# A Fourier mixing layer and a leaky-ReLU MLP on one core: the first rows of x loaded in fp32, loads and banks reordered, and one more chunk computed by Strassen

## The chip, the core and the metric

The kernel runs on one core of one Trainium2 chip. The metric is the device time of one execution in microseconds (us), the median of several runs. TensorE (PE) multiplies matrices and writes its results to PSUM banks. VectorE (DVE), ScalarE (ACT) and GpSimd (POOL) work on tiles. SyncE (SP) and POOL issue the DMA transfers of this kernel, and ACT issues a few at the very end.

## The reference, cut to what matters

```python
def _attn_ref(x, filt_r, filt_i):            # x: (8, 3008, 256) float32
    X = np.fft.rfft(x, axis=1)
    Y = X * (filt_r + 1j * filt_i)[None, :, :]
    return np.fft.irfft(Y, n=x.shape[1], axis=1)

def _moe_ref(x, w_in, w_out):                # x: (24064, 256)
    h = x @ w_in                             # (256, 2048)
    g = np.maximum(0.01 * h, h)
    return g @ w_out                         # (2048, 256)
```

The output of the first function, seen as 24064 tokens, is the input of the second.

## The kernel before, in words

The Fourier transform of length 3008 = 94 x 32 is done as matrix products in fp16, in four stages for each of the eight sequences (`b` = 0 to 7). Stage s1 multiplies the 94 rows of x by a small matrix (`fwd1`). A transposition follows. Stage s2 multiplies by the 24 matrices of `f2_sb`, and the spectrum is multiplied by the filters `fa_sb` and `fb_sb`. Stage sa multiplies by a small inverse matrix, a second transposition follows, and stage sb multiplies by the matrices of `i1_sb` and writes the mixed tokens `yt`. The MLP then works on chunks of 512 tokens: 32 matmuls of 512 columns with `w_in_sb` into the PSUM pair `ph` (L502), a leaky ReLU on ACT (L507) into `gt_c`, and the product with `w_out_sb`. There are 47 chunks.

The second product has two forms. `plain` (L623) does 64 matmuls of 256 columns per chunk (L627) and four copies on DVE (L632). `products` (L595) does Strassen's seven products of half-sized blocks: 112 matmuls of 128 columns (L566), with four sums of activations on DVE (L539), one copy on ACT (L603) and six additions on DVE (L591 to L619). The weight sums `wt_sb` are built once (L655). Chunks below `W0` = 3 are plain, the others Strassen (L711).

The first sequence is a prologue. Its order is written out by hand in the list `FIRST`, step by step: `s1p` matmuls of s1 on rows n0 to n0+n into a bank b0 to b4 (L367), `s1e` the copy of that bank to SBUF on ACT (A) or DVE (D) (L373), `t1` a quarter of the transposition on DVE (L376), `s2p` (L381), then the filter product either directly on DVE (`s2d`, L398) or by a copy on ACT (`s2a`, L401) and a multiplication on POOL (`s2m`, L408), `sap` and `sae` (L413, L418), `t2` (L422), `sbp` and `sbe` (L436, L439), and `warm n`, which issues n matmuls of 512 columns that nobody reads (L362). The banks b0, b1, b2 are single PSUM banks `pf`, b3 and b4 are the pairs `ph`. Each engine runs its own instructions in the order of the list.

What the prologue loads: SP issues the small matrices and two thirds of `f2_sb` (L205 to L207). POOL issues the first sequence of x in four parts of 10, 10, 8 and 4 rows, cast from fp32 to fp16 by the DMA (`x_load`, L188), then the filters with the last third of `f2_sb` between them (L211 to L216), then `w_in_sb`. In the middle of `FIRST` the step `i1` loads `i1_sb` on SP and the step `x` loads the next sequence of x in two halves with `w_out_sb` between them on POOL (`load_x`, L451).

From the second sequence on, the order is made by a planner. Each group of work gets a planned time in units of which 8 are one chunk (`SL`). `PLANS` gives starts and steps of the stages per sequence, `SUMS`, `REST`, `DUE`, `TWICE`, `F2T`, `LEAD`, `AFTER`, `LANDED` give times of single steps and distances between them. A heap sorts them, and the instructions are issued in that order on every engine. A group of s2 (`s2_group`, L293) multiplies one bank by both filters on DVE. In sequence 1 every even group does three DVE operations (L305, L306, L311). The odd groups and all later ones do two (L308, L311) and have two DMAs on SP swap the halves of p2 into p3 (L309, L310). POOL then adds p1 and p3 into y (L314). The tiles p1, p2 and p3 come from the pool `scrp` with two buffers each:

```python
p1, p2, p3 = (scrp.tile([P, 2, D], FP32, tag=f"p{i}", name=f"p{i}_b{b}_g{g}") for i in (1, 2, 3))
```

A group of sa (L321) reads y, its copy goes to ACT (L323), and its store to DRAM to SP (L325). The groups of s1 (L250), s2, sa and sb (L342) share the banks pf0 and pf1 in turn, and DVE and ACT empty them. The transpositions of sequences 1 to 7 go through DRAM (stores L255 and L325, loads L262 and L269).

Of the kernel before, what the change touches and what calls it, by code (L numbers as in the profile page):

```python
# [75 lines left out]
def kernel(  # L76
# [9 lines left out]
    nc = tc.nc  # L86
    B, N, D = x.shape
# [8 lines left out]
    SL = 8  # L96
    NCH = NCT // 2
    QT = 4 * N1
    W0 = 3
    GAP = 0.6  # L100
    EXG = 0
    LANDED = 2.43
    READ = 2.2
    SUMS = (0.09, 1.59, 2.35, 4)
    REST = (5.37, 14.61, 8.86, 10.48, 23.53, 20.72)
    DUE = (3.52, 0.66)
    TWICE = (1.43, 1.84)
    F2T = 3.24
    LEAD = (3.85, 7.37)
    AFTER = (0.53, 0.8, 1.33, 3.17, 0.39, 0.52)  # L110


    PLANS = (
# [4 lines left out]
    )  # L118

    f2_np, i1_np, small_np, f2t_np, i1t_np = _build_np_constants(N)  # L120
    f2_d = nc.inline_tensor(f2_np, name="fwd2_const")
# [6 lines left out]
    f2_sb = cpool.tile([P, NC, P], FP16, name="f2_sb")  # L128
# [5 lines left out]
    w_out_sb = cpool.tile([P, NCT, D], FP16, name="w_out_sb")  # L134
    wt_sb = cpool.tile([P, 4, NCH, P], FP16, name="wt_sb")
    x_sb = cpool.tile([P, N2, D], FP16, name="x_sb")
    big = [cpool.tile([P, Q * D], FP16, name=f"big{i}") for i in range(3)]
# [1 line left out]

    gtp = ctx.enter_context(tc.tile_pool(name="gtp", bufs=2))  # L140
    drp = ctx.enter_context(tc.tile_pool(name="drp", bufs=1, space=bass.MemoryType.DRAM))
    scrp = ctx.enter_context(tc.tile_pool(name="scr", bufs=2))
    ypp = ctx.enter_context(tc.tile_pool(name="ypp", bufs=4))
    outp = ctx.enter_context(tc.tile_pool(name="outst", bufs=4))
    psp = ctx.enter_context(tc.tile_pool(name="psp", bufs=1, space=bass.MemoryType.PSUM))
# [29 lines left out]
    def noted(what, f):  # L175
        f()
        issued.add(what)

    def soon(delay, f):
        at(clock["now"] + delay, f)  # L180
# [7 lines left out]
    def x_load(b, n0=0, nn=N2, d0=0, dn=D):  # L188

        for lo, cnt in ((0, R1),) if b + 1 < B else ((0, 64), (64, N1 - 64)):  # L190
            nc.gpsimd.dma_start(
                x_sb[lo : lo + cnt, ds(n0, nn), ds(d0, dn)],
                bass.AP(tensor=x.tensor, offset=x.offset + (b * N + lo * N2 + n0) * D + d0,
                        ap=[[N2 * D, cnt], [D, nn], [1, dn]]))
# [7 lines left out]
                        ap=[[N1 * D, N2 // 2], [sgn * NC * D, 2], [sgn * D, NC], [1, dn]]))  # L202


    nc.sync.dma_start(small_sb[:], small_d.ap())  # L205
    for i in (1, 0):
        nc.sync.dma_start(f2_sb[:, ts(i, NC // FP), :], f2_d.ap()[i])  # L207
    first_parts = ((0, 10), (10, 10), (20, 8), (28, 4))
    for n0, nn in first_parts:
        x_load(0, n0, nn)  # L210
    for hf in range(2):  # L211

        filt_load(0, filt_r, hf * DH, DH)
        filt_load(64, filt_i, hf * DH, DH)
        if hf == 0:
            nc.gpsimd.dma_start(f2_sb[:, ts(2, NC // FP), :], f2_d.ap()[2])  # L216
    nc.gpsimd.dma_start(w_in_sb[:], moe_w_in.rearrange("(dt p) c -> p dt c", p=P))
    idle = cpool.tile([P, CH], FP16, name="idle")
    nc.vector.memset(idle[:], 0.0)
# [25 lines left out]
    def s1_group(b, g, copy):  # L245
        def go():
# [43 lines left out]
    def y_delay(b, g):  # L290
        return 1.2 if b == 1 and g % 2 == EXG else AFTER[2] if b > 1 else AFTER[3]

    def s2_group(b, g):  # L293
        def go():
# [12 lines left out]
            else:  # L307
                nc.vector.tensor_tensor(p2[:], ps, fb, AL.mult)  # L308
                soon(AFTER[1], lambda: nc.sync.dma_start(p3[0:64], p2[64:P]))  # L309
                soon(AFTER[1], lambda: nc.sync.dma_start(p3[64:P], p2[0:64]))  # L310
            nc.vector.tensor_tensor(p1[:], ps, fa, AL.mult)  # L311
# [5 lines left out]
    def sa_group(b, g):  # L317
        def go():
# [5 lines left out]
            if g % 2:  # L324
                soon(AFTER[4], lambda: noted(("st2", b, h), lambda: nc.sync.dma_start(  # L325
                    dz2[b % 2][ds(4 * h, 4)].rearrange("k p d -> p k d"), st2[h % 4])))
# [29 lines left out]
    engine = {"A": act, "D": dve}  # L356
# [91 lines left out]
        nc.vector.memset(i1_sb[:, 0, 0:2], 0.0)  # L448
        nc.sync.dma_start(i1_sb[:], i1_d.ap())

    def load_x():  # L451

        x_load(1, 0, N2 // 2)
        nc.gpsimd.dma_start(w_out_sb[:], moe_w_out.rearrange("(ct p) d -> p ct d", p=P))
        x_load(1, N2 // 2, N2 // 2)
        issued.add(("x", 1, 0))

    FIRST = """
        warm 18, s1p 0 0 2 b0, s1e 0 0 2 A, s1p 0 2 4 b3, s1p 0 6 4 b4, s1e 0 2 4 D, warm 4, s1p 0 16 4 b3,
        s1e 0 16 4 D, s1p 0 10 2 b1, s1e 0 6 4 A, s1p 0 12 4 b4, s1e 0 10 2 A, warm 2, s1p 0 24 2 b2,  # L460
        s1e 0 12 4 A, s1e 0 24 2 D, s1p 0 20 4 b3, s1e 0 20 4 A, s1p 0 26 2 b0, s1p 0 28 2 b1,
        s1p 0 30 2 b2, s1e 0 26 2 D, s1e 0 28 2 A, s1e 0 30 2 D, t1 1, t1 0, warm 14, s2p 0 0 4 0 b0,
        s2p 0 0 4 1 b1, s2p 0 16 4 0 b2, t1 2, t1 3, s2a 0 0 4 0, s2m 0 0 4 0, s2a 0 0 4 1, s2p 0 16 4 1 b0,
        s2p 0 8 8 0 b4, s2p 0 8 8 1 b3, s2a 0 16 4 0, s2m 0 16 4 0, s2a 0 16 4 1, s2m 0 16 4 1,
        s2p 0 4 4 0 b1, s2d 0 8 8 0, s2p 0 20 4 1 b2, s2d 0 8 8 1, i1, s2d 0 4 4 0, s2p 0 4 4 1 b0,
        s2p 1 8 8 0 b4, s2d 0 4 4 1, warm 1, s2p 1 8 8 1 b3, s2a 1 8 8 0, s2m 0 0 4 1, sap 0 8 b1,
        s2a 1 12 8 0, s2p 1 16 8 0 b4, s2d 0 20 4 1, sap 0 16 b0, s2m 1 12 8 0, x, s2a 1 8 8 1, s2m 1 8 8 1,
        s2d 1 16 8 0, sae 0 8 A, s2a 1 12 8 1, sae 0 16 A, s2p 0 20 4 0 b2, sap 0 4 b1, s2m 1 12 8 1,
        s2p 1 16 8 1 b3, sap 0 0 b0, s2p 1 0 8 1 b4, s2d 0 20 4 0, s2d 1 16 8 1, sae 0 4 A, s2m 1 8 8 0,
        sae 0 0 A, sap 0 20 b1, s2d 1 0 8 1, sap 0 12 b2, s2p 1 0 8 0 b3, sap 1 16 b0, sae 0 20 A,  # L470
        sae 0 12 A, sap 1 12 b1, s2d 1 0 8 0, sap 1 20 b2, t2 0, sap 1 8 b4, t2 1, sae 1 16 A, sap 1 4 b0,
        sap 1 0 b3, sae 1 12 A, warm 5, sbp 0 1 b1, sae 1 20 A, sae 1 8 A, sbp 0 4 b2, sae 1 4 A, sae 1 0 A,
        t2 3, sbp 0 5 b4, sbe 0 1 A, sbp 0 2 b0, t2 2, sbe 0 4 A, sbp 0 6 b3, sbe 0 5 A, sbp 0 7 b1,
        sbp 0 0 b2, sbp 0 3 b4, sbe 0 6 A, sbp 1 1 b3, sbe 0 0 D, sbe 0 2 A, sbp 1 0 b0, sbe 0 3 A,
        sbe 0 7 A, sbe 1 1 D, sbe 1 0 A
    """
    steps = dict(s1p=s1p, s1e=s1e, t1=t1, s2p=s2p, s2d=s2d, s2a=s2a, s2m=s2m, sap=sap, sae=sae, t2=t2,
                 sbp=sbp, sbe=sbe, i1=load_i1, x=load_x, warm=keep_warm)
    for step in FIRST.split(","):
        what, *args = step.split()  # L480
        steps[what](*(int(v) if v.isdigit() else v for v in args))
# [205 lines left out]
    while queue:  # L687
        time, n, stage, b, g, f = heapq.heappop(queue)
# [16 lines left out]
    for ci in range(NCHUNK + 1):  # L705
# [45 lines left out]
```

## Time and profile before

| what | value |
|---|---|
| median of 5 runs | 753.18 us (751.88 to 754.24) |
| the profiled execution's own time | 753.18 us |
| its span, first to last instruction | 751.4 us |
| granted TensorE clock | 0.998 |
| PE busy | 739.0 us, 98% of the span |
| ACT, DVE, POOL busy | 558.9, 499.3, 167.0 us |
| first MLP matmul | 35.12 us after the span's start |

The span and the own time differ by 1.8 us, which lie outside of the instructions. PE is busy from start to end, but its first 35 us belong to the prologue, and a part of these are `warm` matmuls. In the timeline each line has the start, the duration, the engine, the line of the kernel, the operation, the tiles and shapes, how many instructions were merged, and in brackets how long the engine was idle before it and what ended that.

### The profile page before, as it was taken

To read this page: it belongs to the slowest core of one execution; us is meant where nothing else is said; L and a number is where in the kernel's file an instruction comes from. 1 tells how busy PE (TensorE), PEld (TensorE's weight loads), DVE (VectorE), ACT (ScalarE), POOL (GpSimd) and SP (SyncE) were. 2 spreads that over 40 slices of the span, in tenths; PEclk is the share of its full clock that TensorE was granted. 3 is DMA by queue.
4 is the path that set the end of the run, shared out by engine and by line. 5 is a ranking of instruction groups with operands and counts; after the bars stand their busy time and mean duration, and the time that the engine had idled before them with its cause. 6 is when DMAs were issued, how large, how long until landed. Compare 5 with 4: busy or idle time off the path is not lost.

```text
span 751.4 us, 19384 instructions
## 1 busy us (share of the span) xinstructions
PE 739.0 (98%) x8016; PEld 529.1 (70%) x8016; DVE 499.3 (66%) x683; ACT 558.9 (74%) x755; POOL 167.0 (22%) x169
## 2 busy tenths in 40 slices
PE   9999999999999999999999999999999999999997
PEld 3555667767777777877778777777777777777775
DVE  5886645777767775767666657766677576465565
ACT  4775787888878787787777787787777777777662
POOL 5503320342222312221233222222212210000000
PEclk9999999999999999999999999999999999999999
DMA  9976788887876557656676655544554333111011
GB/s 192 228 217 174 179 198 245 201 190 196 216 198 170 142 168 209 144 151 152 188 177 171 155 156 168 154 140 116 142 155 122 105 106 106 51 55 54 29 52 62
DMA packets 119688, 113.34 MB, mean 151 GB/s; under 512 B 16352, under 2 KB 92768, under 8 KB 119408
## 3 DMA queue, kind: packets, MB, share of 16 engines
q1 hardware_dynamic: 104447, 95.36, 42.9%
q0 software_dynamic: 14864, 16.49, 15.8%
q8 instruction: 62, 1.02, 0.6%
q10 hardware_dynamic: 289, 0.26, 0.1%
q14 instruction: 26, 0.21, 0.1%
HBM read 57.51 MB, written 50.33 MB: 144 GB/s over the span
## 4 chain that ended last, share of the span: by engine, by line
PE 92%; DMA 2%; DVE 2%; POOL 2%; issue 0%; SPq 0%; ACT 0%; DVEq 0%
PE ph L502 41%; PE po_ps L566 18%; PE pf L566 18%; PE pf L250 3%; PE pf L342 3%; PE pf L321 2%; PE pf L299 2%; PE po_ps L364 1%; PE po_ps L627 1%; DMA p_b_g<-p_b_g 1%; PE pf L627 1%; POOL prod L396 1%; DMA dz<-big 1%; PE pf L433 0%; DVE big L539 0%
## 5 line engine op out<-in xcount | busy, mean ns | idle before, releaser
L507 ACT ACTIVATE gt_c<-ph 128x1024 f16<-128x1024 f32 x376 | 385.4, 1025 | 135.0 <-PE ph L502 124.3
L502 PE MATMUL ph<-yt,w_in_sb 128*128 128x512 f16 (+7 forms) x1728 | 447.2, 351 | 0.4 <-DVE yt L332 0.4
L566 PEld LDWEIGHTS <-gt_c 128*128 128x128 f16 x2800 | 202.2, 98 | 91.1
L314 POOL TENSOR_TENSOR y_b_g<-p_b_g,p_b_g 128x512 f16<-128x512 f32 x84 | 118.8, 1416 | 415.9 <-DMA p_b_g<-p_b_g 214.1
L566 PEld LDWEIGHTS <-big 128*128 128x128 f16 x2128 | 151.3, 98 | 61.6 <-issue 0.2
L502 PEld LDWEIGHTS <-w_in_sb 128*128 128x128 f16 x1728 | 137.5, 98 | 20.9 <-issue 2.0
L308 DVE TENSOR_TENSOR p_b_g<-pf,fb_sb 128x512 f32<-128x512 f32 x78 | 53.7, 689 | 32.2 <-PE pf L299 14.7
L566 PE MATMUL po_ps<-wt_sb,gt_c 128*128 128x128 f16 x704 | 70.0, 219 | 0.0
L566 PE MATMUL pf<-wt_sb,gt_c 128*128 128x128 f16 x688 | 68.4, 219 | 0.1
L566 PE MATMUL pf<-w_out_sb,gt_c 128*128 128x128 f16 x720 | 67.9, 219 | 0.0
L566 PE MATMUL po_ps<-wt_sb,big 128*128 128x128 f16 x720 | 67.4, 219 | 0.1
L566 PE MATMUL pf<-wt_sb,big 128*128 128x128 f16 x704 | 67.2, 219 | 0.0
L253 ACT CAST big<-pf 128x512 f16<-128x512 f32 x100 | 58.3, 588 | 11.9 <-PE pf L250 10.5
L566 PE MATMUL po_ps<-w_out_sb,gt_c 128*128 128x128 f16 x688 | 66.0, 219 | 0.0
L332 ACT CAST yt<-pf 128x376 f16<-128x376 f32 x120 | 56.4, 473 | 12.4 <-PE pf L342 9.1
L311 DVE TENSOR_TENSOR p_b_g<-pf,fa_sb 128x512 f32<-128x512 f32 x84 | 57.3, 682 | 1.3 <-POOL y_b_g L314 1.1
L539 DVE TENSOR_TENSOR big<-gt_c 128x2048 f16<-128x2048 f16 (+1 forms) x46 | 57.1, 1242 | 0.1
L539 DVE TENSOR_TENSOR gt_c<-gt_c 128x2048 f16<-128x2048 f16 x43 | 55.5, 1291 | 1.0
L539 DVE TENSOR_TENSOR big<-big,gt_c 128x2048 f16<-128x2048 f16 (+1 forms) x45 | 54.8, 1217 | 0.1
L539 DVE TENSOR_TENSOR big<-gt_c,big 128x2048 f16<-128x2048 f16 (+1 forms) x45 | 54.3, 1207 | 0.0
L323 ACT CAST big<-pf 128x512 f16<-128x512 f32 x84 | 49.0, 584 | 5.7 <-PE pf L321 3.9
L250 PE MATMUL pf<-x_sb,small_sb 94*128 94x512 f16 x112 | 42.7, 381 | 0.8 <-DVE big L253 0.8
(85 smaller groups left out, 618.0 us busy)
## 6 DMA issues: line engine op xcount, KB each, us to landing
dz<-big SPq DMA_DIRECT2D x98, 256.0 KB
p_b_g<-p_b_g SPq DMA_DIRECT2D x156, 128.0 KB
out_dram<-ost_c_h SPq DMA_DIRECT2D x119, 128.0 KB
big<-dz SPq DMA_DIRECT2D x42, 256.0 KB
big<-dz SPq DMA_DIRECT2D x56, 192.0 KB
x_sb<-in_x_dram POOLq DMA_DIRECT2D x41, 192.0 KB, 4.5
x_sb<-in_x_dram POOLq DMA_DIRECT2D x2, 768.0 KB, 13.2
w_in_sb<-in_moe_w_in_dram POOLq DMA_DIRECT2D x1, 1024.0 KB, 13.9
```

The lines of the kernel that those rows point to most:

```text
L250: nc.tensor.matmul(ps, fwd1[:N1], x_sb[:N1, ds(2 * g, 2), :], start=True, stop=True)
L253: copy(st[:, ds(2 * (g % 2), 2), :], ps)
L308: nc.vector.tensor_tensor(p2[:], ps, fb, AL.mult)
L311: nc.vector.tensor_tensor(p1[:], ps, fa, AL.mult)
L314: ("y", b, g), lambda: nc.gpsimd.tensor_tensor(y1[:], p1[:], p3[:], AL.add)))
L323: nc.scalar.copy(st2[h % 4][:, ds(2 * (g % 2), 2), :], ps)
L332: copy(yv, ps.rearrange("p c a -> p a c"))
L342: nc.tensor.matmul(ps[:, j, :], z2[h % 4][:K4, j, ts(dt, P)], i1_sb[:K4, 4 * h + j, :], start=True, stop=True)
L502: nc.tensor.matmul(ph[:, j, ds(t - ci * CH, e - t)], w_in_sb[:, dt, ts(ct, P)], yt[:, dt, ds(t % N, e - t)], start=(dt == 0), stop=(dt == ...
L507: nc.scalar.activation(gts[ci][:, ds(2 * g, 2), :], ph, AF.Lrelu)
L539: nc.vector.tensor_tensor(*(v[:, ds(c0, n)] for v in (o, i0, i1)), op)
L566: nc.tensor.matmul(po[:, t], a()[:, c, ts(t, P)], w[:, c, :], start=(c == 0), stop=(c == NCH - 1))
```

## The change

It has four parts. First, six rows of x are loaded by SP in fp32 into the memory of `big[1]` (`x_early`) and rounded to fp16 by ACT and DVE (step `xc`); the other 26 rows come in three casting DMAs of 10, 10 and 6 rows. Second, two thirds of `f2_sb` are loaded on SP from inside `FIRST` (step `f2`), each after a tiny DVE memset that orders it. The first third is loaded by POOL right behind x. `i1` stands later in the list. The loads of the next x are two steps, and `w_out_sb` follows the second. Third, `scrp` has three buffers. Fourth, `W0` is 2, so that chunk 2 is a Strassen chunk. The order of `FIRST` and the planner's constants are new throughout.

```diff
-    W0 = 3
+    W0 = 2
-    LANDED = 2.43
+    LANDED = 2.22
-    SUMS = (0.09, 1.59, 2.35, 4)
-    REST = (5.37, 14.61, 8.86, 10.48, 23.53, 20.72)
-    DUE = (3.52, 0.66)
-    TWICE = (1.43, 1.84)
-    F2T = 3.24
-    LEAD = (3.85, 7.37)
-    AFTER = (0.53, 0.8, 1.33, 3.17, 0.39, 0.52)
+    SUMS = (0.12, 1.44, 2.82, 4.06)
+    REST = (5.94, 11.49, 9.04, 11.18, 24.01, 16.48)
+    DUE = (3.43, 0.63)
+    TWICE = (2.2, 2.35)
+    F2T = 3.11
+    LEAD = (4.09, 5.91)
+    AFTER = (0.67, 0.29, 1.73, 3.11, 0.1, 0.67)
     PLANS = (
-        (0.68, 0.31, 12.95, 0.9, 4.35, 38.33, 2.78, 7.78, 1.61),
-        (12.19, 1.53, 42.87, 2.62, 7.4, 85.59, 2.85, 16.13, 2.12),
-        (40.7, 1.73, 77.28, 3.57, 5.62, 130.03, 2.65, -0.23, 2.52),
-        (63.95, 2.85, 119.86, 3.87, 7.04, 177.42, 2.92, 12.93, 2.24),
+        (0.68, 0.02, 12.06, 0.92, 3.62, 38.87, 2.77, 3.81, 1.63),
+        (12.54, 1.57, 43, 2.58, 7.22, 84.56, 2.9, 17.19, 2.09),
+        (40.86, 1.72, 76.21, 3.47, 5.87, 131.4, 2.68, -0.71, 2.65),
+        (64.1, 2.89, 120.34, 3.87, 7.18, 177.35, 2.92, 10.66, 2.51),
     )
-    scrp = ctx.enter_context(tc.tile_pool(name="scr", bufs=2))
+    scrp = ctx.enter_context(tc.tile_pool(name="scr", bufs=3))
+    EARLY = 6
+    x_early = big[1][:].bitcast(FP32)[:, : EARLY * D].rearrange("p (n d) -> p n d", n=EARLY)
     nc.sync.dma_start(small_sb[:], small_d.ap())
-    for i in (1, 0):
-        nc.sync.dma_start(f2_sb[:, ts(i, NC // FP), :], f2_d.ap()[i])
-    first_parts = ((0, 10), (10, 10), (20, 8), (28, 4))
-    for n0, nn in first_parts:
+    nc.sync.dma_start(x_early[:R1], bass.AP(tensor=x.tensor, offset=x.offset, ap=[[N2 * D, R1], [D, EARLY], [1, D]]))
+    for n0, nn in ((6, 10), (16, 10), (26, 6)):
         x_load(0, n0, nn)
+    nc.gpsimd.dma_start(f2_sb[:, : NC // FP, :], f2_d.ap()[0])
...
-        if hf == 0:
-            nc.gpsimd.dma_start(f2_sb[:, ts(2, NC // FP), :], f2_d.ap()[2])
...
-    def load_x():
-        x_load(1, 0, N2 // 2)
+    def load_f2(i):
+        nc.vector.memset(f2_sb[:, i * NC // FP, 0:2], 0.0)
+        nc.sync.dma_start(f2_sb[:, ts(i, NC // FP), :], f2_d.ap()[i])
+
+    def load_x(half):
+        x_load(1, half * N2 // 2, N2 // 2)
+        issued.add(("x", 1, 0))
+
+    def load_w_out():
         nc.gpsimd.dma_start(w_out_sb[:], moe_w_out.rearrange("(ct p) d -> p ct d", p=P))
-        x_load(1, N2 // 2, N2 // 2)
-        issued.add(("x", 1, 0))
+
+    def round_x(n0, n, e):
+        engine[e](x_sb[:N1, ds(n0, n), :], x_early[:N1, ds(n0, n), :])
     FIRST = """
-        warm 18, s1p 0 0 2 b0, s1e 0 0 2 A, s1p 0 2 4 b3, s1p 0 6 4 b4, s1e 0 2 4 D, warm 4, s1p 0 16 4 b3,
-        s1e 0 16 4 D, s1p 0 10 2 b1, s1e 0 6 4 A, s1p 0 12 4 b4, s1e 0 10 2 A, warm 2, s1p 0 24 2 b2,
-        s1e 0 12 4 A, s1e 0 24 2 D, s1p 0 20 4 b3, s1e 0 20 4 A, s1p 0 26 2 b0, s1p 0 28 2 b1,
-        s1p 0 30 2 b2, s1e 0 26 2 D, s1e 0 28 2 A, s1e 0 30 2 D, t1 1, t1 0, warm 14, s2p 0 0 4 0 b0,
...
+        xc 0 4 A, xc 4 2 D, warm 18, s1p 0 0 4 b3, s1p 0 4 2 b0, warm 3, s1p 0 14 2 b1, s1e 0 4 2 D,
+        s1e 0 0 4 A, s1p 0 10 4 b4, s1e 0 10 4 A, s1p 0 6 4 b3, s1e 0 14 2 D, warm 4, s1p 0 20 4 b4,
+        s1e 0 6 4 D, s1p 0 16 4 b3, s1e 0 16 4 A, s1p 0 26 2 b2, s1p 0 24 2 b0, s1e 0 24 2 A, f2 1,
+        s1e 0 20 4 D, s1p 0 28 2 b1, s1p 0 30 2 b4, s1e 0 26 2 D, s1e 0 30 2 A, s1e 0 28 2 D, t1 0, f2 2, t1 1,
...
```

The last lines of the new `FIRST` hold `x 0` after six of the eight POOL multiplications, and `x 1, w_out` after the eighth; the old one held `x` after the fifth. The numbers of filter products on DVE (ten) and POOL (eight) are the same.

More of the change, by code (lines that the diff above doesn't have):

```diff
@@ L458 @@
     FIRST = """
-        warm 18, s1p 0 0 2 b0, s1e 0 0 2 A, s1p 0 2 4 b3, s1p 0 6 4 b4, s1e 0 2 4 D, warm 4, s1p 0 16 4 b3,
-        s1e 0 16 4 D, s1p 0 10 2 b1, s1e 0 6 4 A, s1p 0 12 4 b4, s1e 0 10 2 A, warm 2, s1p 0 24 2 b2,
-        s1e 0 12 4 A, s1e 0 24 2 D, s1p 0 20 4 b3, s1e 0 20 4 A, s1p 0 26 2 b0, s1p 0 28 2 b1,
-        s1p 0 30 2 b2, s1e 0 26 2 D, s1e 0 28 2 A, s1e 0 30 2 D, t1 1, t1 0, warm 14, s2p 0 0 4 0 b0,
-        s2p 0 0 4 1 b1, s2p 0 16 4 0 b2, t1 2, t1 3, s2a 0 0 4 0, s2m 0 0 4 0, s2a 0 0 4 1, s2p 0 16 4 1 b0,
@@ L464 @@
[L464 to L473, printed above, removed]
@@ L474 @@
-        sbp 0 0 b2, sbp 0 3 b4, sbe 0 6 A, sbp 1 1 b3, sbe 0 0 D, sbe 0 2 A, sbp 1 0 b0, sbe 0 3 A,
-        sbe 0 7 A, sbe 1 1 D, sbe 1 0 A
+        xc 0 4 A, xc 4 2 D, warm 18, s1p 0 0 4 b3, s1p 0 4 2 b0, warm 3, s1p 0 14 2 b1, s1e 0 4 2 D,
+        s1e 0 0 4 A, s1p 0 10 4 b4, s1e 0 10 4 A, s1p 0 6 4 b3, s1e 0 14 2 D, warm 4, s1p 0 20 4 b4,
+        s1e 0 6 4 D, s1p 0 16 4 b3, s1e 0 16 4 A, s1p 0 26 2 b2, s1p 0 24 2 b0, s1e 0 24 2 A, f2 1,
+        s1e 0 20 4 D, s1p 0 28 2 b1, s1p 0 30 2 b4, s1e 0 26 2 D, s1e 0 30 2 A, s1e 0 28 2 D, t1 0, f2 2, t1 1,
@@ new lines @@
+        warm 14, s2p 0 0 4 0 b3, s2p 0 0 4 1 b2, warm 2, s2p 0 8 4 1 b0, s2a 0 0 4 0, s2a 0 0 4 1, t1 3,
+        s2p 0 12 4 1 b4, t1 2, s2d 0 8 4 1, s2p 0 12 4 0 b1, s2p 0 16 8 0 b3, s2m 0 0 4 0, s2m 0 0 4 1,
+        s2d 0 16 8 0, s2a 0 12 4 1, s2p 0 8 4 0 b2, s2p 1 16 8 0 b4, s2p 0 4 4 1 b0, s2a 0 12 4 0, s2d 0 8 4 0,
+        s2a 1 16 8 0, s2p 0 4 4 0 b1, s2p 1 16 8 1 b3, i1, s2d 0 4 4 0, s2a 1 20 8 0, sap 0 8 b2, s2d 0 4 4 1,
+        s2a 1 16 8 1, s2a 1 20 8 1, s2m 0 12 4 0, s2p 0 16 8 1 b4, sap 0 0 b1, s2p 1 0 8 1 b3, s2m 0 12 4 1,
@@ new lines @@
+        sap 0 12 b0, s2m 1 20 8 0, sae 0 8 A, s2d 0 16 8 1, sae 0 0 A, s2p 1 8 8 1 b4, sap 0 4 b2, s2d 1 0 8 1,
+        sap 0 16 b1, sae 0 12 A, s2p 1 8 8 0 b3, sap 0 20 b0, s2d 1 8 8 1, s2m 1 20 8 1, sae 0 4 A,
+        s2d 1 8 8 0, s2p 1 0 8 0 b4, sae 0 16 A, sap 1 20 b2, s2d 1 0 8 0, sap 1 12 b1, sae 0 20 A, sap 1 8 b0,
+        x 0, s2m 1 16 8 0, sae 1 20 A, s2m 1 16 8 1, x 1, w_out, sae 1 12 A, sae 1 8 A, sap 1 16 b3,
+        sae 1 16 A, sap 1 4 b2, t2 1, sae 1 4 A, sap 1 0 b4, t2 0, sae 1 0 A, warm 4, sbp 0 1 b1, sbp 0 4 b0,
@@ L476 @@
+        sbp 0 0 b3, sbp 0 3 b2, t2 3, sbe 0 1 A, sbe 0 4 A, sbe 0 0 A, sbp 0 2 b4, sbp 0 7 b1, sbp 0 6 b0,
+        t2 2, sbe 0 2 A, sbe 0 7 A, sbp 0 5 b3, sbp 1 0 b4, sbp 1 1 b1, sbe 0 6 A, sbe 0 5 A, sbe 1 1 A,
+        sbe 0 3 D, sbe 1 0 D
     """
     steps = dict(s1p=s1p, s1e=s1e, t1=t1, s2p=s2p, s2d=s2d, s2a=s2a, s2m=s2m, sap=sap, sae=sae, t2=t2,
-                 sbp=sbp, sbe=sbe, i1=load_i1, x=load_x, warm=keep_warm)
+                 sbp=sbp, sbe=sbe, i1=load_i1, f2=load_f2, x=load_x, w_out=load_w_out,
+                 xc=round_x, warm=keep_warm)
```

## The prediction

> **What bounds the kernel now.** I read the page first, then the timeline of the first 80 us, then PE's waits, then single tiles, and last the order in which both built programs issue on each engine. From the page:
>
> ```profile
> span 751.4 us, 19384 instructions
> PE 739.0 (98%) x8016; PEld 529.1 (70%) x8016; DVE 499.3 (66%) x683; ACT 558.9 (74%) x755; POOL 167.0 (22%) x169
> ...
> L502 PE MATMUL ph<-yt,w_in_sb 128*128 128x512 f16 (+7 forms) x1728 | 447.2, 351 | 0.4 <-DVE yt L332 0.4
> ```
>
> PE is the bound, and the start times of its matmuls show no slack inside: two 512-column matmuls start 216 ns apart, two of 256 columns 109, two of 128 columns 56. Summing the 7708 matmuls from the first MLP matmul on at these spacings gives 704.1 us. From 35.12 us to PE's end at 745.9 there are 710.7 us, so only 6.6 us are stalls. Three things can change the time: when the first MLP matmul starts, the stalls, and the matmuls themselves.
>
> The prologue, from the timeline (start, duration, engine, line, idle before):
>
> ```profile
> 8.05 0.38 PE L370 MATMUL pf<-x_sb,small_sb 94*128 94x512 f16 x1
> 12.25 2.05 DVE L279 CAST big<-pf 128x512 f16<-128x512 f32 x3 [0.21 <-PE pf L370]
> 14.40 4.62 DVE L379 STREAM_TRANSPOSE big<-big 128x1024 f32<-128x1024 f32 x4
> 17.92 5.65 POOL L396 TENSOR_TENSOR prod<-spare,fa_sb 128x512 f16<-128x512 f32 x5 [2.02 <-ACT spare L406]
> 24.11 1.18 POOL L454 DMA_DIRECT2D w_out_sb<-in_moe_w_out_dram  x1
> 25.82 3.39 POOL L396 TENSOR_TENSOR prod<-spare,fa_sb 128x512 f16<-128x512 f32 x3
> 29.27 0.59 PE L416 MATMUL ph<-prod,small_sb 128*128 128x512 f16 x2 [0.30 <-POOL prod L396]
> 31.52 2.37 DVE L425 STREAM_TRANSPOSE big<-big 128x1024 f32<-128x1024 f32 x2 [0.58 <-ACT big L419]
> 35.12 1.07 PE L502 MATMUL ph<-yt,w_in_sb 128*128 128x512 f16 x4 [0.41 <-DVE yt L332]
> ```
>
> From 14.40 to 33.89 DVE works without a gap but for 0.11 and 0.58 us: four transposes, ten filter products, four transposes. So the start of t1 sets the first MLP matmul. POOL, held 2.3 us by DMA issues, costs the 0.58. PE's stalls after that:
>
> ```profile
> 39.55 0.38 PE L250 MATMUL pf<-x_sb,small_sb 94*128 94x512 f16 x1 [0.33 <-DVE big L253]
> 42.17 0.38 PE L250 MATMUL pf<-x_sb,small_sb 94*128 94x512 f16 x1 [0.51 <-DVE big L253]
> 67.50 0.38 PE L299 MATMUL pf<-big,f_sb 128*128 128x256 f16 x2 [0.97 <-DVE p_b_g L311]
> 72.22 0.38 PE L321 MATMUL pf<-y_b_g,small_sb 128*128 128x512 f16 x1 [0.65 <-DVE p_b_g L311]
> 113.80 0.35 PE L342 MATMUL pf<-i_sb,big 96*128 96x94 f16 x4 [1.37 <-DMA big<-dz]
> ```
>
> By start times they cost 0.49, 0.67, 1.14, 0.81 and 1.54 us, 4.65 together; none is left after 121 us beyond 0.23. The two in the middle are sequence 1's filter groups on DVE:
>
> ```profile
> 61.68 0.69 DVE L305 TENSOR_TENSOR p_b_g<-pf,fb_sb 64x512 f32<-64x512 f32 x1
> 64.89 0.41 DVE L632 COPY ost_c_t<-pf 128x256 f32<-128x256 f32 x1
> 66.75 0.69 DVE L311 TENSOR_TENSOR p_b_g<-pf,fa_sb 128x512 f32<-128x512 f32 x1
> 71.47 0.69 DVE L311 TENSOR_TENSOR p_b_g<-pf,fa_sb 128x512 f32<-128x512 f32 x1 [0.54 <-POOL y_b_g L314]
> ```
>
> DVE needs 5.8 us without pause for groups 0, 1, a copy and group 2, then group 3 gets its bank. The last line waits for a buffer that POOL still reads.
>
> **What the Trainium skill says.** "TensorE: Matmul & The Clock Gate", section "Back-to-back issue gap", gives N / 2.4 + 2.5 ns per warm matmul of N columns; the trace agrees (216, 109, 56). "DMA: Bandwidth & Descriptors", "SWDGE vs HWDGE vs iDMA", says that only transfers issued by GpSimd can cast, and that a DMA engine alternates between its queues: the packet records agree, with one SP packet of 96 ns between two casting x packets of 398 ns. On buffers and waits no page bears beyond this.
>
> **Part by part.** Times T+ count from the first MLP matmul along PE's new order at the spacings above.
>
> *Early rows and f2 order.* Removed: one casting part, two f2 transfers ahead of x. Added: SP's x_early (96 packets of 6144 B, 234 ns each by the later f2 load, six per engine, 1.4 us of transfer), two casts, one `warm` more (0.22 us, in a wait). Before, x landed at 7.33, 9.93, 11.79 and 12.68 us. At 398 ns per 5120 B packet I estimate x_early at 5.5, the others near 7, 9.4 and 11. The cast of 94x1024 on ACT I take at 1.0 us (L507's 1025 ns), bounds 0.5 and 2; DVE's half of it less. Both end before 7.8, under the 18 warm matmuls that still hold PE until 8.05. If that cover went, each us would delay s1 by one.
> The bank order then decides. A copy starts 0.42 us after its last matmul starts; four rows take 1.03 to 1.09 us on ACT, 1.22 on DVE, two rows 0.6 and 0.69. Rows 0 to 3 are ready at 8.69, ACT frees b3 at 9.76; rows 6 to 9 follow in b3, ready at 10.64; DVE frees b3 at 11.86; rows 16 to 19 are ready at 12.56, and ACT copies 16 to 19, 24 and 25, 30 and 31 until 14.75. DVE ends at 14.45. t1 starts at 14.8, not at 14.40: the x that lands earlier is not used. The same sum for the old order gives its 14.40.
> f2's two memsets (0.06 us each) lie in DVE's queue; f2 parts 1 and 2, two SP issues of 0.4 us, have 3 us before their use. POOL's f2 part 0 lands behind x near 11.6, needed at 17. The filters keep their place, all bytes being the same.
>
> *x, w_out, i1 behind.* Three POOL issues (0.59 + 1.18 + 0.54 us) leave the chain; one of 0.59 stays before the last two of eight multiplications of 1.13. POOL starts near 18.4 and ends near 28, DVE's products end at 29.5. So POOL no longer stops DVE: 0.5 us gained. t2 ends at 14.8 + 18.8 (DVE's work without gaps) + 0.3 (memsets, short gaps) = 33.9, as before. Start of the MLP: **0** (range -0.9 to +0.8). The moved transfers are hidden: at the 411 GB/s (fp32 side) at which DMA ran from 22 to 42 us, x half 0 lands near 33 (needed T+0.9 = 36), half 1 near 37 (T+6.5), w_out near 42 (T+10.5 = 45.6), i1 by 30.5 (needed 32). SP's queue has nothing behind i1 until the stores at T+2.8; behind w_out on POOL stand x loads of sequence 2, needed at T+20. If w_out came 4 us late, PE would stand for it.
>
> *TWICE spread* (0.95 us DVE operations every 2.35 units, not 1.84, the first behind group 2's copy): retracing DVE's queue, the banks come free in time; 0.15 us remain of 1.16. **-1.0**.
>
> *Three buffers; sequence 1 earlier in PE's order.* The wait for POOL at 71.47 goes: -0.81. But groups 2 and 3 stand at T+26.49 and 28.46 instead of 27.03 and 29.43, while DVE still needs until T+30.45 to empty group 2: the stall grows from 1.14 to 2.05. Group 0 is due at sa at T+29.65, its y ready at 28.2. Behind the waiting L299 stand all MLP matmuls. **+0.1**.
>
> *Chunk 2 by Strassen.* 64 matmuls at 109 ns become 112 at 56: **-0.72**. DVE gets four sums of 1.22, six additions and loses four copies of 0.42 between T+44 and T+62, where groups 8 to 11 still run. The first sum (1.24) stands before group 8, which frees its bank at T+49.93 with the earlier stall counted, while PE wants it at 49.2; the second sum delays group 9, wanted at 51.75, to 52.4; group 10 adds 0.15. **+1.6** (bounds 0 and +3: the trace of before has no Strassen chunk beside these groups).
>
> *Second transposition.* From the last sa matmul to the first sb there were 9.63 us plus a stall of 1.54, so it takes 11.17; now 9.80 are planned: stall 1.37. Sequence 2 has 10.76 against 11.36: up to 0.4. **0** (-1.4 to +1). Later sequences keep 12 us and more.
>
> Sum: 0 - 1.0 + 0.1 - 0.72 + 1.6 + 0 = 0.0 us. The profiled execution took 753.18 us (span 751.4, 1.8 outside), which is also the median, so I predict 753.2.
>
> **Rivals.** *DVE becomes the bound in sequence 1* (slower). It decides when a group's bank is late by more than counted: should ACT's last leaky ReLU of chunk 2 or a POOL y hold the sums or L305, everything on DVE's queue slips and PE with it. For it: DVE has 15 us of work in T+44 to T+60. Against: DVE was idle 1 to 3 us at a time in the same stretch before. Two such slips of 1 to 2 us: 756.
> *The early x is used* (faster). Copies run at ACT's and DVE's rate and t1 starts at 13.5, 0.9 earlier, and the planner's spacing holds, so that group 3 and chunk 2 cost 0.7 rather than 1.6 and 0.9 more: 753.2 - 0.9 - 1.5 = 750.8. For it: every x part lands 1 to 2 us ahead. Against: the bank chain above.
> *The change doesn't do what it says*: w_out, last in POOL's queue, lands behind the stores and PE waits 1 to 2 us for its first plain matmul: 754.7.
>
> **How the numbers follow.** About 0.2% (1.5 us) can be told from no change. My sum 0.40, own range 751.7 to 754.7; slower cases 0.31, mostly the first rival; faster 0.29. The range 750.2 to 756.6 leaves out one in ten on each side.
>
> **What would show it.** Right: t1 (L379) at 14.8 with x landed by 11.5; L416's wait on POOL gone; first L511 at 35.1; no L250 stall near T+4; L299 waiting for DVE L311 2 us near T+28.5 and again near T+47; 64 L636 fewer, 112 L575 more. Wrong: t1 before 14.0 or after 15.5, a wait of L636 for w_out, or stalls beyond 120 us.

## The result, and the profile after

The changed kernel takes 757.83 us (median of 25 runs, 753.18 to 759.93) against 753.25 us for the kernel before (45 runs, 751.75 to 756.50): 1.0049 times as long by the means of all runs, 95% interval 1.0039 to 1.0060. That is slower by 0.5%, where I had forecast no change, and the median lies above my range. The 25 times fall into two groups, and the median stands at the edge between them: 12 between 753.2 and 756.8 us (median 755.2), 13 between 757.8 and 759.9 (median 758.7). Even the lower group is slower than before. PE's mean granted clock was 0.994 to 0.997 in every run of the upper group and 0.998 or more in all but one of the lower. The profiled execution (758.07 us, clock 0.997) is of the upper one.

From the page of the changed kernel:

```profile
span 755.9 us, 19503 instructions
PE 740.4 (98%) x8065; PEld 530.0 (70%) x8065; DVE 510.1 (67%) x693; ACT 559.8 (74%) x756; POOL 168.2 (22%) x168
...
L511 PE MATMUL ph<-yt,w_in_sb 128*128 128x512 f16 (+7 forms) x1728 | 448.5, 352 | 0.2 <-ACT yt L332 0.2
```

PE is still the bound. Its matmuls should have become 0.72 us cheaper and yet PE is busy 1.4 us longer. The line of the first MLP layer shows the same: 448.5 us for the same 1728 matmuls that took 447.2. Some of them ran slowly, as the stalls below show.

The prologue, from the timeline (start, duration, engine, line, idle before):

```profile
14.55 2.42 DVE L379 STREAM_TRANSPOSE big<-big 128x1024 f32<-128x1024 f32 x2 [0.30 <-ACT big L279]
15.76 0.06 DVE L453 MEMSET f_sb<- 128x1 uint32 x1
21.27 0.64 PE L388 MATMUL ph<-big,f_sb 128*128 128x128 f16 x8 [1.99 <-DMA f_sb<-fwd_const]
22.01 1.23 DVE L396 TENSOR_TENSOR prod<-ph,fa_sb 128x1024 f16<-128x1024 f32 x1 [2.21 <-PE ph L388]
31.03 4.70 DVE L425 STREAM_TRANSPOSE big<-big 128x1024 f32<-128x1024 f32 x4
36.72 0.38 PE L511 MATMUL ph<-yt,w_in_sb 128*128 128x512 f16 x1 [0.25 <-ACT yt L332]
```

The first transposition starts at 14.55, close to the 14.8 I had worked out. The memset at 15.76 is the step `f2 2`. Its transfer is issued then, and PE waits for it until 21.27. VectorE, which sets the end of the prologue, then stands idle for 2.2 us behind PE. The first MLP matmul comes at 36.72 instead of 35.12. One execution can mislead by half a microsecond here. Over the profiles of all runs, this start is at 35.12 to 36.10 in the four kernels with the old prologue (mean 35.5), and at 36.05 to 36.77 in the four where PE waits for f2 at the full clock (mean 36.4).

The stalls after that, from the timeline of the same execution:

```profile
68.88 0.38 PE L299 MATMUL pf<-big,f_sb 128*128 128x256 f16 x2 [1.37 <-DVE p_b_g L311]
88.22 0.38 PE L299 MATMUL pf<-big,f_sb 128*128 128x256 f16 x2 [0.33 <-DVE p_b_g L311]
90.55 0.38 PE L321 MATMUL pf<-y_b_g,small_sb 128*128 128x512 f16 x1 [0.42 <-DVE p_b_g L311]
97.39 1.17 SPq L310 DMA_DIRECT2D p_b_g<-p_b_g  x1
97.91 1.03 POOL L191 DMA_DIRECT2D x_sb<-in_x_dram  x2
102.10 0.59 PE L511 MATMUL ph<-yt,w_in_sb 128*128 128x512 f16 x2
103.22 2.23 POOL L314 TENSOR_TENSOR y_b_g<-p_b_g,p_b_g 128x512 f16<-128x512 f32 x1 [4.29 <-DVE big L548]
105.51 0.38 PE L321 MATMUL pf<-y_b_g,small_sb 128*128 128x512 f16 x1 [2.54 <-POOL y_b_g L314]
105.83 1.01 PE L511 MATMUL ph<-yt,w_in_sb 128*128 128x512 f16 x2
```

The first three are the waits that I had foreseen: group 3 and the groups beside chunk 2's sums. The one at 105.51 is new. PE wants y of group 11 and stands idle for 2.70 us by start times. The y is late because the second half of its swap (L310) was issued at 97.39, its last packet ended at 102.53 and POOL began to add at 103.22, when VectorE's sum L548 (101.86 to 103.08) was over; the addition then took 2.23 us. In the kernel before, with the swap issued from 94.56 to 95.68 and its last packet at 97.16, the same two loads of x came after it:

```profile
96.24 1.03 POOL L191 DMA_DIRECT2D x_sb<-in_x_dram  x2
97.66 1.27 POOL L314 TENSOR_TENSOR y_b_g<-p_b_g,p_b_g 128x512 f16<-128x512 f32 x1 [0.39 <-PE ph L502]
```

What I had not looked for stands in the last line of the list before. Two MLP matmuls take 0.59 us at 102.10 and 1.01 us after the stall. The trace's record of the granted clock has it at half from 105.87 to 109.28. By start times this costs another 1.65 us.

Set out like the prediction's sum, with both profiled executions cut at the same places (times after; PE's start-to-start times less the spacing of its matmuls):

| part | predicted us | measured us |
|---|---|---|
| start of the MLP | 0 | +1.60 |
| first 23 us of it (TWICE spread, L250) | -1.0 | -0.46 |
| groups 0 to 4 of sequence 1, 60 to 76 us | +0.1 | +0.38 |
| matmuls (chunk 2 by Strassen) | -0.72 | -0.72 |
| stalls beside chunk 2's sums, 76 to 100 us | +1.6 | +1.14 |
| group 11's y, 100 to 112 us: 2.70 idle, 1.65 at half rate | not priced | +4.35 |
| second transposition, 112 to 130 us | 0 | -1.56 |
| the rest | 0 | -0.19 |
| sum | 0 | +4.5 (755.9 less 751.4) |

### The profile page after: what moved, and what is told of

It is laid out like the page before. It is cut to its first block, busy times and chain, and to the rows that moved or that the text cites. A ratio compares the mean times of both kernels' runs of the same rounds, so it can differ in the third digit from the quotient of the medians.

```text
span 755.9 us, 19503 instructions
## 1 busy us (share of the span) xinstructions
PE 740.4 (98%) x8065; PEld 530.0 (70%) x8065; DVE 510.1 (67%) x693; ACT 559.8 (74%) x756; POOL 168.2 (22%) x168
## 4 chain that ended last, share of the span: by engine, by line
PE 86%; DVE 1%; POOL 0%; issue 0%; DVEq 0%; POOLq 0%
PE ph L511 40%; PE pf L575 18%; PE po_ps L575 18%; PE pf L342 3%; PE pf L250 3%; PE pf L321 2%; PE pf L299 2%; DVE big L548 0%; POOL y_b_g L314 0%; DVE ost_c_h L600 0%; DVE ost_c_h L608 0%; DVE p_b_g L311 0%; DVE big L618 0%; DVEq L615 0%; POOLq L314 0%
## 5 line engine op out<-in xcount | busy, mean ns | idle before, releaser
L511 PE MATMUL ph<-yt,w_in_sb 128*128 128x512 f16 (+7 forms) x1728 | 448.5, 352 | 0.2 <-ACT yt L332 0.2
L575 PEld LDWEIGHTS <-gt_c 128*128 128x128 f16 x2864 | 207.5, 98 | 96.5 <-issue 3.8
L575 PEld LDWEIGHTS <-big 128*128 128x128 f16 x2176 | 155.6, 98 | 63.5 <-issue 0.7
L575 PE MATMUL po_ps<-wt_sb,gt_c 128*128 128x128 f16 x720 | 71.7, 219 | 0.0
L575 PE MATMUL pf<-wt_sb,gt_c 128*128 128x128 f16 x704 | 71.6, 219 | 0.0
L575 PE MATMUL pf<-wt_sb,big 128*128 128x128 f16 x752 | 71.4, 219 | 0.0
L575 PE MATMUL po_ps<-w_out_sb,gt_c 128*128 128x128 f16 x752 | 71.2, 219 | 0.0
L253 ACT CAST big<-pf 128x512 f16<-128x512 f32 x100 | 58.2, 583 | 7.1 <-PE pf L250 5.6
L548 DVE TENSOR_TENSOR big<-gt_c 128x2048 f16<-128x2048 f16 (+1 forms) x47 | 59.4, 1264 | 0.0
L548 DVE TENSOR_TENSOR big<-big,gt_c 128x2048 f16<-128x2048 f16 (+1 forms) x46 | 59.1, 1284 | 0.1
L548 DVE TENSOR_TENSOR gt_c<-gt_c 128x2048 f16<-128x2048 f16 x44 | 57.1, 1297 | 1.1
L311 DVE TENSOR_TENSOR p_b_g<-pf,fa_sb 128x512 f32<-128x512 f32 x84 | 57.2, 681 | 0.2
L548 DVE TENSOR_TENSOR big<-gt_c,big 128x2048 f16<-128x2048 f16 (+1 forms) x46 | 55.8, 1212 | 0.0
L250 PE MATMUL pf<-x_sb,small_sb 94*128 94x512 f16 x112 | 42.9, 383 | 0.0
```

The source lines that it names most:

```text
L250: nc.tensor.matmul(ps, fwd1[:N1], x_sb[:N1, ds(2 * g, 2), :], start=True, stop=True)
L253: copy(st[:, ds(2 * (g % 2), 2), :], ps)
L511: nc.tensor.matmul(ph[:, j, ds(t - ci * CH, e - t)], w_in_sb[:, dt, ts(ct, P)], yt[:, dt, ds(t % N, e - t)], start=(dt == 0), stop=(dt == ...
L548: nc.vector.tensor_tensor(*(v[:, ds(c0, n)] for v in (o, i0, i1)), op)
L575: nc.tensor.matmul(po[:, t], a()[:, c, ts(t, P)], w[:, c, :], start=(c == 0), stop=(c == NCH - 1))
```

## Experiments

Theory A: f2 part 2 is issued too late, and group 11's y has too short a lag, after which PE's clock is halved. Theory C, added to A: x loads that GpSimd issues beside group 11's swap hold the swap up. Rival B: VectorE is the bound beside chunk 2's sums. Ratios are to the kernel before, run again beside each experiment, with 95% intervals. "Stalls" are PE's start-to-start excess from the first MLP matmul to the last, 6.4 us before and 10.1 after.

**f2 part 2 earlier**

```diff
-  ... s1e 0 24 2 A, f2 1, s1e 0 20 4 D, ... t1 0, f2 2, t1 1,
+  ... s1e 0 24 2 A, f2 1, f2 2, s1e 0 20 4 D, ... t1 0, t1 1,
```

> The changed kernel with one step moved: f2 part 2 is loaded directly behind f2 part 1 (issue near 12.2 us, not 15.8). Theory A (a transfer on SP's queue amid the filter load needs 3.7 us to its first packet, so it has to be issued earlier): part 2 lands before 18, PE's L388 no longer waits 2.0 us at 21.27, t2 (L425) starts near 29.4 instead of 31.03, first L511 near 35.1 instead of 36.72; the total falls by 1.6 us against the changed kernel. Rival (the filters are as late as f2, so DVE's products wait for fa next): t2 stays after 30.5 and the total stays within 0.5 us.

Measured: 754.29 us, ratio 1.0017 (1.0008 to 1.0025), 3.5 us below the changed kernel. From its timeline:

```profile
14.05 4.62 DVE L379 STREAM_TRANSPOSE big<-big 128x1024 f32<-128x1024 f32 x4 [0.30 <-ACT big L279]
28.30 4.71 DVE L425 STREAM_TRANSPOSE big<-big 128x1024 f32<-128x1024 f32 x4
33.98 1.18 PE L511 MATMUL ph<-yt,w_in_sb 128*128 128x512 f16 x4 [0.22 <-ACT yt L332]
102.67 0.38 PE L321 MATMUL pf<-y_b_g,small_sb 128*128 128x512 f16 x1 [2.54 <-POOL y_b_g L314]
```

The wait is gone, and the MLP starts at 33.98: 2.7 us earlier than after, and 1.1 earlier than in the kernel before. So the repaired prologue gains; in the four kernels that have it the start is at 33.98 to 34.62 (mean 34.3). The stall at group 11 is the same 2.70 us, but this time the matmuls behind it run at the full rate. The same idle time halves the clock in one execution and not in another.

The clock records show where the two differ. In all 13 profiles the clock changes only on marks that are 3.41 us apart, counted from its first rise to full speed. Here are the stretches between these marks (from and to, length, PE busy with its matmuls, granted clock, share and rate of the DMA). First the changed kernel, then this one:

```profile
102.46:105.87 3.41, 0.87 (x11) 1.00 0.90 258
105.87:109.28 3.41, 3.41 (x21) 0.50 0.76 105
98.05:101.46 3.41, 2.09 (x23) 1.00 1.03 279
101.46:104.87 3.41, 2.19 (x23) 1.00 0.43 68
```

In the changed kernel the whole 2.70 us lie in one stretch, and the next one runs at half clock. Here a mark divides them into 1.49 and 1.21 us, and the clock stays.

**The lag of sequence 1 alone**

```diff
-        (0.68, 0.02, 12.06, 0.92, 3.62, 38.87, 2.77, 3.81, 1.63),
+        (0.68, 0.02, 12.06, 0.92, 4.35, 38.87, 2.77, 3.81, 1.63),
```

> The changed kernel with only the lag of sequence 1's plan put back to 4.35. In PE's order group 11's filter matmul stands 8.3 us of matmuls before its inverse matmul instead of 7.2. Theory A (group 11's y is late because 7.2 us are too few for its products, swap, and POOL's sum, and a stall of 2.7 us then halves PE's clock for 3 us more): the stall at L321 shrinks to 1.6 us, no matmul at half rate follows, L342 waits about 1 us instead; total 2 to 3 us less than the changed kernel's slower executions (about 755.5 to 756.5). Rival B (VectorE's sums for chunk 2 are what loses the time, wherever the groups stand): within 1 us of the changed kernel.

Measured: 757.94 us, 1.0065 (1.0051 to 1.0079). The stall at group 11 fell to 1.45 us without half rate, as A says, but the total did not fall. The new order lost as much elsewhere, most of it in one line of its timeline:

```profile
86.56 0.49 PE L575 MATMUL po_ps<-w_out_sb,gt_c 128*128 128x128 f16 x6 [1.72 <-DVE ost_c_t L641]
```

With filter groups 8 and 9 earlier in VectorE's queue, the copy L641 that frees an output bank for chunk 2 stands behind three filter products. The stalls between 76 and 100 us were 3.81 instead of 1.42, so this run does not show what a longer lag alone is worth. My expectation of 755.5 to 756.5 missed this; the lag is no free parameter.

**The x loads beside the swap**

```diff
-                at(s1 + xl + x_step * g, lambda g=g: ...
+                at(max(s1 + xl + x_step * g, 37.5 if b == 2 else 0) - 4 * (b == 1 and g == 15), lambda g=g: ...
```

> The changed kernel with two loads of x moved on GpSimd's queue: they stood between y of group 10 and y of group 11 and were issued at 97.9 us, while the swap of group 11's product was being issued; now one is issued before group 9's y and one after group 11's. PE's and VectorE's order is the same. Theory C (the packets of these casting loads hold up the swap's second half, which came first 1.9 us after its issue ended, and so the y): the swap's packets end near 100.5 instead of 102.2, y starts by 101, the stall at L321 falls from 2.7 to under 1 us with no matmul at half rate; total 2.5 to 4 us less. Theory A alone (too short a lag, y slowed to 2.2 us by VectorE's sums): swap and stall change by less than 0.7 us, total within 1 us or by chance out of the slower mode.

Measured: 756.12 us, 1.0042 (1.0026 to 1.0058). From its timeline:

```profile
21.04 1.04 PE L388 MATMUL ph<-big,f_sb 128*128 128x128 f16 x8 [2.02 <-DMA f_sb<-fwd_const]
98.65 1.65 SPq L310 DMA_DIRECT2D p_b_g<-p_b_g  x1
102.33 1.27 POOL L314 TENSOR_TENSOR y_b_g<-p_b_g,p_b_g 128x512 f16<-128x512 f32 x1 [3.09 <-PE pf L321]
104.08 0.38 PE L321 MATMUL pf<-y_b_g,small_sb 128*128 128x512 f16 x1
```

C is shown: the issue of the swap's second half ends at 100.30 and POOL adds at 102.33, 2.0 us later, where the changed kernel needed 4.7 (98.56 to 103.22). This half also took longer to issue here, so I count from the issue of the first half as well: 4.2 us instead of 6.4, which is 2.2 us gained. The packet records say the same: the last packets of this half come by 101.9, 1.6 us after the issue, not by 102.5, 4.0 us after it. The addition takes 1.27 us, and PE does not wait. Stalls are 6.8 us instead of 10.1. The total fell only 1.7 us, and this execution shows a loss in the prologue. Eight matmuls after the wait for f2 take 1.04 us, not 0.64: PE's clock was halved there (20.94 to 24.35), and the MLP starts at 37.81. The mean clock of five of the six executions was 0.996 or 0.997, so most may have lost there.

**Chunk 2 plain again** (`W0 = 3`)

> The changed kernel with chunk 2 as four plain products again (W0 = 3). Theory A: 0.72 us of matmuls come back; without VectorE's sums beside them POOL's y of groups 9 to 11 takes 1.27 us instead of 1.8 to 2.2, the stalls between 85 and 95 us (1.4 us) go, the one at group 11 falls to 1 to 1.7 us and no half rate follows; L342 then waits 1 to 1.5 us (8.9 us stand between the last inverse matmul and the first of the final stage). Total near 755. Rival B (VectorE's sums cost it all): no stall is left at group 11, total 753.5 to 754.

Measured: 757.16 us, 1.0050 (1.0033 to 1.0067).

```profile
96.97 1.03 POOL L191 DMA_DIRECT2D x_sb<-in_x_dram  x2
97.47 0.59 SPq L310 DMA_DIRECT2D p_b_g<-p_b_g  x1
103.77 1.75 POOL L314 TENSOR_TENSOR y_b_g<-p_b_g,p_b_g 128x512 f16<-128x512 f32 x1 [5.77 <-DMA p_b_g<-p_b_g]
```

The stalls between 76 and 100 us go (1.42 to 0.13), so the sums cost 1.3 us for the 0.72 they save. But group 11 still waits 2.5 us, for the swap beside the two x loads, and half clock follows (4.19 us between 100 and 112). B falls as the cause of the large stall: without the sums it stays. My figure of 755 missed, because I had put part of the late y down to the sums.

**One part at a time on the kernel before.** The changed prologue alone:

> The kernel before with the changed prologue only (early fp32 rows, f2 part 0 behind x, parts 1 and 2 by steps, the new written order, x, w_out and i1 where the change puts them); plan, buffers, spread and Strassen as before. Theory A: f2 part 2 is issued near 15.8 us and lands near 21.2, the first MLP matmul starts at 36.7 (37.8 where PE's clock drops during that wait) instead of 35.1, and the stalls after it are those of before (6.4 us), since lag and order are unchanged: 754.8 to 756. Rival (the prologue is no loss; the whole loss comes after it): within 0.5 us of before.

Measured: 754.50 us, 1.0021 (1.0005 to 1.0038); L387 waits 2.0 us for f2, the MLP starts at 36.05, stalls 6.8. The prologue costs 1.2 us. The rival, no loss beyond 0.5 us, is just inside the interval of the total (0.4 to 2.9 us), but the wait and the later start speak against it. The four executions with a mean clock of 0.998 or more took 753.0 to 754.5 us, the three with 0.996 took 755.6 to 756.1. Three product buffers alone (`bufs=3`):

> The kernel before with three product buffers only. Theory A: VectorE's L311 of group 3 no longer waits for POOL, the stall of 0.81 us at L321 (71.30) goes, the one of 1.13 at L299 stays: 752.3 to 752.6. Rival (the wait for the buffer moves on: the swap or y of the group is as late, or the next group's bank waits): within 0.2 us of before.

Measured: 752.61 us, 0.9987 (0.9979 to 0.9994). The stall at 72.22 is gone and that at L299 is 1.12: 0.8 gained, as reckoned. Chunk 2 by Strassen alone (`W0 = 2`):

> The kernel before with chunk 2 by Strassen only (W0 = 2). Theory A: 0.72 us of matmuls less; stalls of 1.3 us between 80 and 95 us beside VectorE's sums, as the changed kernel lost against its variant with W0 = 3; group 11 stands 9.4 us before its inverse matmul, so no stall over 1 us there; total 0.3 to 1 us above before. Rival (the sums and POOL's slower y take group 11's y beyond 9.4 us): stall of 1 us or more at L321 near 100 us and 2 to 4 us above before.

Measured: 756.06 us, 1.0042 (1.0029 to 1.0056); stalls between 76 and 100 us 3.34 instead of 0.28, nearly all on VectorE's L311, and none at group 11. The total is as high as the rival had it, without the rival's stall; theory A had the place right and less than half the size. With the groups where they stood before, the sums cost 3.1 us there, and a further 1.2 us of stalls come after 130 us, the largest 0.78 at 544.6. What these are was not looked into.

**PE's clock after a stall of known length**

```diff
+    def probe(k):
+        ps = bank("pf", 1, CH)[:, 0]
+        nc.tensor.matmul(ps, idle[:, 0:P], idle[:], start=True, stop=True)
+        for _ in range(k):
+            nc.vector.tensor_copy(probe_sb[:], ps)
+        nc.tensor.matmul(bank("pf", 1, CH)[:, 0], probe_sb[:, 0:P], idle[:], start=True, stop=True)
+    for i in range(16):
+        at(SL * (12 + 2 * i) + 0.26, lambda i=i: probe((1, 2, 3, 4, 5, 2, 3, 4, 3, 4, 2, 3, 4, 3, 6, 8)[i]))
```

> The kernel before with 16 stalls of known length put into PE's stream, one in each second chunk from 12 on: a matmul into a free bank, k copies of it by VectorE one after the other (0.69 us each), a matmul that reads the copy; k is 1 to 6 and 8. Nothing else waits for them. Theory (PE's clock is halved after an idle stretch whose length alone decides, with some chance in its phase): after stalls under 2 us (k = 1, 2) the next matmuls are at the full rate; after 2.5 to 3.3 us (k = 3, 4) some run at half rate for about 3 us and some don't; after 4 us and more (k = 5, 6, 8) all do. Each such stretch costs 1.5 to 1.7 us. Rival (the half rate after group 11's stall comes from the transfers or the power there): no half rate after any of them.

Measured: 851.68 us, one execution. The stalls came out longer than k copies, since other work was ahead of the copies on VectorE. By start times, and cut at the 3.41 us marks of the clock:

| idle us | most idle us between two marks | half rate after it |
|---|---|---|
| 1.81 | 1.0 | no |
| 3.11 | 1.6 | no |
| 2.57, 2.61, 3.12 | 2.6 to 3.1 | yes, cost 1.65 to 1.68 |
| 3.33 to 6.78 (11 stalls) | 2.1 to 3.4 | yes each time, cost 1.4 to 2.8 |

By the clock records half rate lasts one, two or, after the longest stall, three whole stretches of 3.41 us, and it begins on a mark. So idle time alone halves the clock; no special transfer or place is needed, and the length alone, as my theory had it, does not decide. Stalls of 61.4 us, 30.3 us at half rate and 6.9 us of added matmuls add up to 98.6, against 98.3 measured.

**Both repairs in the changed kernel**

> The changed kernel with both repairs: f2 part 2 directly behind part 1, and no x load between y of groups 10 and 11. Theory A with C: first MLP matmul at 34.0, no stall at group 11, 0.8 us at L342, 6.5 us of stalls in all; span 749.6, total 751.4. Rival (the time only moves: an earlier start meets other transfers, and new waits of 1 us or more come up in sequence 1): total as with f2 alone moved, 754.3.

Measured: 752.54 us, 0.9990 (0.9982 to 0.9998): 5.3 us below the changed kernel. MLP start 34.62, no stall at group 11, 1.07 us at L342, stalls 7.2. I had expected 1.1 us less; 0.6 of it is the start.

**The parts that gain, on the kernel before**: prologue with f2 part 2 behind part 1, three buffers, TWICE = (2.2, 2.35); plan and plain chunk 2 as before.

> The kernel before with the repaired prologue (f2 part 2 behind part 1), three product buffers and the change's spread of the filter doublings; plan and plain chunk 2 as before. From the parts measured: first MLP matmul at 34.0; 704.1 us of matmuls; stalls 6.4 less 0.5 for L250 less 0.8 for the wait on POOL, 5.1; span 748.9, total 750.8. Rival (with 3 buffers or the earlier start the stall at L299 or at L342 takes the gain back): 752 to 753.

Measured: 750.48 us, 0.9966 (0.9954 to 0.9978), faster than both kernels. MLP start 34.14, stalls 5.6. PE's largest stalls that are left are 1.4 us for the second transposition, 1.1 for group 3's bank and 0.8 at L249.

**The same with chunk 2 by Strassen**

> The kernel of repaired prologue, three buffers and new spread, with chunk 2 by Strassen as well. Theory A (the sums beside groups 8 to 11 cost PE more than the 0.72 us that they save, even with three buffers and 9.4 us for group 11's y): stalls of 1.3 to 2 us between 80 and 95 us, 0.6 us less at L342 (10.2 us instead of 9.6 before it), total 0 to 0.7 us above the same kernel with plain chunk 2, 750.5 to 751.2. Rival (with three buffers and the longer lag Strassen is all gain): stalls there under 0.5 us, total 749.5.

Measured: 753.96 us, 1.0005 (0.9995 to 1.0016): 3.5 us worse. From its timeline:

```profile
85.35 0.38 PE L298 MATMUL pf<-big,f_sb 128*128 128x256 f16 x2 [0.49 <-DVE p_b_g L310]
87.55 2.32 DVE L547 TENSOR_TENSOR big<-big,gt_c 128x2048 f16<-128x2048 f16 x1
92.40 0.38 PE L298 MATMUL pf<-big,f_sb 128*128 128x256 f16 x2 [0.78 <-DVE p_b_g L310]
```

Between 76 and 100 us the stalls are 2.96 instead of 0.18. The rest is a start 0.3 us later and 1.0 us of stalls after 100 us, less the 0.72 of matmuls. A sum of 1.22 us takes 2.32 while POOL adds two y beside it. The Trainium skill, "GPSIMD Engine Reference", section "1. Specifications", says that GpSimd shares its SBUF interfaces with VectorE and contends with VectorE instructions of two SBUF inputs. The traces fit: POOL's y takes 1.27 us alone and up to 2.3 beside a sum. Neither theory had the size.

## Why the prediction missed

*Early rows and bank order*: right for t1, wrong for x. The three casting parts landed at 8.32, 10.60 and 12.38 us, where I had put 7, 9.4 and 11, so the last came only 0.3 us before that of the kernel before. The banks set t1 as worked out: 14.55 here, and 13.6 to 14.6 in the nine profiled kernels with this order of copies. With the wait for f2 out of the way, VectorE's chain from t1 to the end of t2 took 19.0 us (14.05 to 33.01) against my 19.1.

*"f2 parts 1 and 2, two SP issues of 0.4 us, have 3 us before their use"*: **the first step that failed.** Part 2 was issued at 15.8, its first packets came at 19.7 and PE had it at 21.27, 5.4 us after the issue. I had used the rule that a DMA engine alternates between its queues ("DMA: Bandwidth & Descriptors", "SWDGE vs HWDGE vs iDMA") and taken alternation to mean a prompt start. The packet records show alternation only once SP's packets are there. With the filters' 256-byte packets running on GpSimd's queue, SP's came first 3.9 us after both issues, and 3.9 after the earlier issue in the repaired kernel. In the kernel before, SP issued f2 at 1.18, before GpSimd's queue moved anything, and its first packet came 1.2 us later. The first half of group 11's swap (L309, issued at 96.86) had its first packet after 1.1. What holds them was not tried. Of 0, the step became +1.6 in the profile, and the repair gave back 2.7 there; by the means of four profiles each it is +0.9 and 2.1.

*x, w_out and i1 behind*: right in that L416 no longer waits for POOL and no L636 waits for w_out. But here VectorE was late itself; in two of the four kernels with the repaired prologue L416 waits 0.4 us for POOL again.

*TWICE spread*: right in direction, half the size. L250's two stalls went, but L433 now waits 0.45 for the bank that ACT's L253 empties: -0.46 for -1.0.

*Three buffers; sequence 1 earlier*: the buffer's 0.8 was right. The stalls up to group 3 were 2.3 by start times (0.43, 0.36, 1.53), 2.05 foreseen. **The second step that failed** is its last sentence: I checked that y of group 0 comes in time, and no other. In PE's new order group 11 has 7.2 us of matmuls between its two matmuls instead of 9.4, and it needed 9.9 (95.63 to 105.51): its swap competed with two x loads, and its sum with VectorE's. That is 2.70 us, with the half rate 4.35, and the largest term of all. That moving the x loads cures it is shown, with the same lag; a longer lag alone did not.

*Chunk 2 by Strassen*: -0.72 exact, +1.1 of stalls for +1.6, inside the bounds. The net loss that I forecast (+0.9) is real (+0.4 here), and larger where the groups keep their old places.

*Second transposition*: 1.37 foreseen, none seen, because PE lost 4.35 us just before, while ACT's and SP's work went on. With group 11 repaired the stall is back (0.84 and 1.07).

The rivals: VectorE's overload was not the main cause, since the stall at group 11 stays without the sums. "The early x is used" came true in part, and only with the repaired prologue: its four profiles start t1 at 13.6 to 14.5 where four profiles with the old prologue have 14.4 to 14.8, and the MLP by the means 1.2 us earlier; 0.8 of that is gained behind t1. Without the 4.35 of group 11 the measured terms sum to 0.2, but the second transposition's -1.56 hangs on it. With the stall of a_xl there (0.92 instead of 1.61 us between 112 and 130) the sum is about 1.1.

## What to carry to other kernels

When an order is made tighter, list the slack of every consumer, not that of the first: here group 0 was fine and group 11 decided. Give a transfer on another queue its time from issue to landing as seen beside the same traffic, and ask which loads are issued within a microsecond or two of a small transfer that somebody waits for. A PE stall of more than 2 us may cost another 1.7 us at half clock.

## What the runs showed of the hardware

PE's half rate after idling was the surprise. The Trainium skill, "TensorE: Matmul & The Clock Gate", section "HAM oscillation — how this bites in real kernels", gives the rule of no PE-idle gaps above about 3.4 us. Here stalls of 2.51 (plain chunk 2), 2.57, 2.61 and 2.70 us were followed by half rate, while one of 3.11 and another of 2.70 were not. The page's free-running window ("What's actually happening") explains this, and the traces agree with it: the clock changes on marks 3.41 us apart. But a window need not be idle throughout. I added up PE's idle time, by start times, between each two marks. Of 2817 such stretches at full clock in the 13 profiles, the 17 with 2.13 us or more of idle time were each followed by half clock, and the 2800 with 1.98 us or less by full clock. In the prologue, where PE works in short bursts, the short gaps count too: 2.32 us halved the clock with the x loads moved, 1.88 in the changed kernel did not. So by these runs a single stall under 2 us is safe where PE is dense, one over 4.3 us, twice 2.13, is not, and between them it depends on where the marks fall.

This can make a kernel's times fall into groups, since one such stretch costs about 1.7 us in some executions and not in others. It accounts for only a part of the 3.5 us between the two groups of the changed kernel. The profiled execution had one such stretch and a mean clock of 0.997; from this I estimate one or two of them for the upper group's 0.994 to 0.997. What else separates the groups is not shown, since no trace of the lower one was kept.
